# A new order list and a new list of PSUM tiles for an attention and expert kernel

## The chip, the cores and the metric

The kernel runs on one core of one Trainium2 chip. The metric is the device time of one execution in microseconds, as the median of the runs; a second kind of run records a profile, and all rows below come from one such execution.

## The reference, cut to what matters

Four batches with eight heads, 768 tokens, 64 numbers per head. Queries and keys are hashed to six bits with a common projection; a query sees only the keys whose six bits equal its own. The masked softmax attention of the 32 heads is put side by side to rows x of 512 numbers. Then, in each batch, the 128 tokens with the largest score x . w_gate pass through an expert (512 to 1024, relu, 1024 to 512), weighted with the sigmoid of the score, and are added to their own rows.

```python
q_bits = (np.einsum('bhsd,dk->bhsk', q, proj) > 0)
mask = q_bucket[:, :, :, None] == k_bucket[:, :, None, :]
scores = np.where(mask, scale * q @ k.T, -1e9)
out = softmax(scores) @ v
...
top_idx = np.argpartition(-(x[b] @ w_gate), capacity)[:capacity]
ye = np.maximum(xe @ w1, 0.0) @ w2
out[b, top_idx] = xe + sigmoid(score) * ye
```

## The kernel before

The whole program is written out as a list of words (ORDER). A loop at the end of `body` takes them one after the other; a word `name.h.i` calls one small function, for example `s.5.2` the score matmuls of head 5, unit 2. Each call puts its instructions behind those already in the queue of its engine, so the list fixes the sequence of every engine (TensorE, VectorE, ScalarE, GpSimd) and of both DMA queues in use (SP and ScalarE's own). Engines wait for each other by semaphores where data or a buffer asks for it; nothing is reordered when it runs. Words `w`, `c0` to `c3`, `e0` to `e3` each run a generator on to its next `yield`: weight loads, the choice of the tokens of a batch, the expert of a batch.

A second list, BANKS, gives to each new PSUM tile, in the sequence of the words that ask for one, one of four places: three tiles of two banks (numbers 0 to 2) and one of a single bank (3). Large results (max words, score words with even unit, hashes) need two banks, the others fit anywhere. A matmul that writes into a place waits until its last user has been read.

What the words do, by head h:

- `X` loads the transposed queries and keys (SP; the first two heads half by SP and half by ScalarE's queue), `xh` (ScalarE, L431) and `xl` (VectorE, L436) split them into two float16 parts. `V` loads values (ScalarE's queue), `vh` and `vl` split them. `lp` loads the projection and `pq` (VectorE, L336) splits it.
- `hx` (head 0, L382) and `h` (the others, L349) are hash matmuls; `sx`, `sg` take signs; `hs`, `dd` place signs and rows into the tile A for head 0, `ps` and `pa` do it by DMA on SP for the others (L443). `pb` copies into the tile B by DMA on SP. A has five buffers and B four, so `pa.h` and `ps.h` wait for the last score matmul of head h-5, `pb.h` for that of head h-4.
- `kv` (VectorE, L555) subtracts halves of the keys, `mx` (TensorE, L563), `re` (ScalarE, L570), `ma` (TensorE, L579) and `rd` (VectorE, L589) find the maximum of each query's scores. `mt` (TensorE, L597) transposes the maxima, `mc2` (ScalarE, L602) copies them, `mr` (SP, L443) writes them as a row into A. For head 0 `rt` and `rk` do this without a DMA.
- `s` (TensorE, L623 and L626) are the score matmuls, six units per head, and need the row; `e` (ScalarE, L639, L643) is the exponential; `r` (VectorE, L656) or `g` (GpSimd, L659) take the part that bfloat16 lost; `a` (TensorE, L683), six per head, multiplies with the values, 18 matmuls each.
- `rc` and `nw` (VectorE, L693 to L721) normalise, `sv`, `sh`, `sl`, `sa`, `sk`, `sd` prepare the start value of the sums. `sc` computes gate scores of the last batch.
- `c0` to `c2`: scores on VectorE, a transpose on TensorE, a copy, store and load back through HBM on SP (`sbc`), ranks by comparing, `idx` (VectorE, L848) and an indirect gather by GpSimd (L853). `c3` does the last batch without HBM.
- `e0` to `e2`: transposes of the gathered rows (TensorE, L875), up matmuls (L915; a step has 12), relu (ScalarE L926, VectorE L927, called htl), down matmuls (L937), the weighted sum (L949) and a scatter (L953). `e3` is the same for the last batch, fed by a selection with matmuls (L1073); `zh` and `zl` (VectorE, L1103) split x for it.
- `wu.30` (L273) are 30 matmuls on constants, `wl` (L1108) four on weights; their results are not used.

How the list before came about does not stand in the kernel; no cost and no due time is part of the program.

Of the kernel before, what the change touches and what calls it, by code (L numbers as in the profile page):

```python
# [52 lines left out]
rd.1.0 e.0.1 s.0.0 s.0.2 s.0.3 vh.1 ps.3.1 mt.1 e.0.0 e.0.2 pb.1.0 mc2.1 vl.1 X.4 ps.3.0 s.0.4 kv.2 e.0.3 mx.2.2  # L53
e.0.4 mx.2.1 s.0.5 r.0.0 a.0.0 w pb.1.1 w re.2.1 mr.1 mx.2.0 a.0.1 ma.2.1 re.2.2 ma.2.2 X.5 e.0.5 s.1.5 kv.3
rd.2.1 pa.3.0 rd.2.2 X.6 X.7 re.2.0 pb.2.3 xh.4 pb.2.2 pb.3.2 pb.3.3 e.1.5 g.0.1 pa.4.0 ma.2.0 s.1.2 pb.3.0 w sv.1
ia.4 mx.3.2 rd.2.0 a.0.2 wl.1 r.0.2 pb.2.1 xh.5 re.3.2 e.1.2 ma.3.2 s.1.0 sh.1 pb.2.0 sa.0 xl.4 sl.1 rd.3.2 xh.6
a.0.3 e.1.0 sk.0 s.1.3 mt.2 xh.7 mc2.2 w xl.5 a.0.4 mr.2 mx.3.1 re.3.1 xl.6 s.1.1 s.1.4 e.1.1 xl.7 r.1.0 w ma.3.1
e.1.4 h.1.0.4 e.1.3 pa.4.1 rd.3.1 a.0.5 mx.3.0 s.2.1 s.2.3 V.2 sg.1.0.4 ss.1.0.4 pa.5.1 re.3.0 e.2.1 rc.0 s.2.2
nw.0 e.2.3 g.1.1 ma.3.0 pb.4.2 w sd.1 rd.3.0 w s.2.5 s.2.0 ps.4.1 pa.5.0 mt.3 e.2.2 a.1.0 e.2.5 a.1.1 s.2.4 w
ps.4.0 ps.6.1 pb.3.1 kv.4 mc2.3 r.1.2 X.8 mx.4.0 mr.3 e.2.0 re.4.0 sa.1 a.1.2 sk.1 mx.4.1 X.9 X.10 ps.5.1 a.1.3  # L60
ma.4.0 a.1.4 re.4.1 ps.5.0 ma.4.1 pb.5.3 r.2.0 w e.2.4 rd.4.0 rd.4.1 a.1.5 xh.8 mx.4.2 pb.5.1 s.3.4 pa.6.0 rc.1
g.2.1 vh.2 s.3.2 re.4.2 ps.7.0 ma.4.2 s.3.5 ps.7.1 nw.1 e.3.4 sd.2 rd.4.2 pa.6.1 kv.5 r.2.2 s.3.0 e.3.5 s.3.3
# [1105 lines left out]
```

## Time and profile before

| | |
|---|---|
| median of 3 runs | 403.53 us (402.72 to 405.96) |
| profiled execution, its own time | 402.91 us |
| its span, first to last instruction | 401.1 us |
| TensorE matmul busy | 380.8 us (95%) |
| VectorE busy | 346.2 us (86%) |
| ScalarE busy | 304.1 us (76%) |
| GpSimd busy | 122.9 us (31%) |
| DMA | 53.82 MB moved, 134 GB/s on average |

Busy time of TensorE counts a matmul until its result is out, and matmuls overlap; so a busy engine can still run with gaps between the starts of its matmuls. Times in the rows are microseconds from the start of the span, durations are microseconds or, in groups, nanoseconds for one instruction.

### The profile page before, as it was taken

The page shows a single profiled execution, that of the slowest core. Times are in us where ns is not written, and L with a number is a line of the kernel's source. Part 1 is how long each engine was busy: PE and PEld are TensorE (multiplying, and loading weights), DVE is VectorE, ACT ScalarE, POOL GpSimd, SP SyncE. Part 2 cuts the span into 40 slices and gives each one's busy share as a digit, 9 for nine tenths or more (in the row PEclk, how much of TensorE's full clock was granted, in tenths as well). Part 3 has the DMA queues.
Part 4 walks back from the last instruction along what each step waited for, and adds up shares of the span by engine and source line. Part 5 has one row for each costly group of instructions (what it writes and reads, how often), then busy time and mean ns, then how long its engine had stood idle before and what let it go on. Part 6 is the DMA issues. An engine that isn't in the chain of part 4 may idle for free. (4 is left out here: it accounts for less than half of the span.)

```text
span 401.1 us, 13734 instructions
## 1 busy us (share of the span) xinstructions
PE 380.8 (95%) x5769; PEld 273.8 (68%) x5775; DVE 346.2 (86%) x580; ACT 304.1 (76%) x483; POOL 122.9 (31%) x80
## 2 busy tenths in 40 slices
PE   1989999999999999899999999999999999999996
PEld 0555677667666867578766677688576776779794
DVE  2779889998998999968899999987989998989942
ACT  3599998978898999779876997958667787784210
POOL 1004335223325234433142224222225235142010
PEclk9999999999999999999999999999999999999999
DMA  7467666475663654473573744332526442020210
GB/s 224 120 193 204 190 193 189 142 195 167 187 203 105 190 167 111 133 210 107 157 239 94 186 113 116 84 80 69 147 59 210 119 115 79 22 82 2 80 50 32
DMA packets 33191, 53.82 MB, mean 134 GB/s; under 512 B 5311, under 2 KB 24266, under 8 KB 33130
## 3 DMA queue, kind: packets, MB, share of 16 engines
q1 hardware_dynamic: 22480, 33.71, 30.2%
q10 hardware_dynamic: 10010, 17.15, 14.0%
q0 software_dynamic: 640, 2.10, 1.7%
q8 instruction: 45, 0.74, 0.8%
q14 instruction: 16, 0.13, 0.1%
HBM read 26.29 MB, written 7.35 MB: 84 GB/s over the span
## 5 line engine op out<-in xcount | busy, mean ns | idle before, releaser
L659 POOL TENSOR_TENSOR R<-P 128x1536 f16<-128x1536 f32 x32 | 88.0, 2749 | 149.5 <-DVE rc L693 34.7
L683 PEld LDWEIGHTS <-P 128*128 128x128 bf16 x2304 | 116.6, 97 | 14.2 <-issue 0.8
L683 PE MATMUL av<-V,P 128*128 128x65 f16 (+1 forms) x2304 | 122.3, 193 | 0.0
L683 PE MATMUL av<-V,R 128*128 128x65 f16 x1152 | 118.0, 192 | 0.3 <-DVE R L656 0.3
L656 DVE TENSOR_TENSOR R<-P 128x1536 f16<-128x1536 f32 x64 | 111.7, 1763 | 0.7 <-ACT P L639 0.6
L643 ACT ACTIVATE P<-two 128x1024 f32<-128x1024 f32 x96 | 97.0, 1022 | 17.5 <-PE two L626 15.1
L683 PEld LDWEIGHTS <-R 128*128 128x128 f16 x1152 | 105.5, 98 | 0.6 <-DVE R L656 0.6
L589 DVE TENSOR_REDUCE m<-two 128x2 fp32r<-128x770 f32 x96 | 89.9, 952 | 13.8 <-PE two L579 11.6
L623 PE MATMUL two<-A 97*128 97x512 f16 (+1 forms) x278 | 93.8, 347 | 1.5 <-DMA A<-mr 0.9
L626 PE MATMUL two<-B 128*128 128x512 f16 (+1 forms) x278 | 93.8, 346 | 0.0
L570 ACT ACTIVATE two<-two 128x770 f32<-128x770 f32 x96 | 75.3, 796 | 9.8 <-PE two L563 8.8
L623 PEld LDWEIGHTS <-A 97*128 97x128 f16 x384 | 37.7, 98 | 27.4 <-DMA A<-mr 3.9
L626 PEld LDWEIGHTS <-B 128*128 128x128 f16 x384 | 37.6, 98 | 23.8 <-issue 3.0
L579 PE MATMUL two<-A 96*128 96x385 f16 x192 | 46.9, 327 | 1.2 <-ACT two L570 0.8
L563 PE MATMUL two<-kd,A 96*128 96x385 f16 x192 | 45.4, 326 | 1.1 <-DVE A L427 0.7
L639 ACT ACTIVATE P<-one 128x512 f32<-128x512 f32 x53 | 31.4, 593 | 7.3 <-PE one L626 7.1
L436 DVE SCALAR_TENSOR_TENSOR XL<-X,XH 128x768 f16<-128x768 f32 x32 | 30.2, 953 | 0.4 <-DMA B<-XL 0.2
L639 ACT ACTIVATE P<-two 128x512 f32<-128x512 f32 x43 | 25.2, 592 | 5.0 <-PE two L626 3.4
L623 PE MATMUL one<-A 97*128 97x256 f16 x106 | 26.3, 273 | 2.5 <-DMA A<-mr 2.4
L431 ACT ACTIVATE XH<-X 128x768 f16<-128x768 f32 x32 | 26.7, 837 | 2.4 <-DMA X<-in_qk_dram 2.3
L626 PE MATMUL one<-B 128*128 128x256 f16 x106 | 26.3, 273 | 0.0
L579 PEld LDWEIGHTS <-A 96*128 96x128 f16 x192 | 16.2, 97 | 11.0 <-issue 2.7
(154 smaller groups left out, 494.4 us busy)
## 6 DMA issues: line engine op xcount, KB each, us to landing
X<-in_qk_dram SPq DMA_DIRECT2D x30, 384.0 KB
V<-in_v_dram ACTq DMA_DIRECT2D x16, 384.0 KB
B<-XL SPq DMA_DIRECT2D x64, 96.0 KB
B<-A SPq DMA_DIRECT2D x64, 96.0 KB
A<-XH SPq DMA_DIRECT2D x62, 96.0 KB
out_dram<-x ACTq DMA_DIRECT2D x7, 768.0 KB
W<-in_w_dram ACTq DMA_DIRECT2D x8, 512.0 KB
sbc<-scores SPq DMA_DIRECT2D x3, 384.0 KB
```

Source lines behind the costliest of these rows:

```text
L436: mine(nc.vector.scalar_tensor_tensor(xl, st["X", h], XS, st["XH", h], op0=ALU.mult, op1=ALU.subtract))
L563: nc.tensor.matmul(pt[:, i, : HS + 1], a[0:96, 0, q0 : q0 + P], kd, start=True, stop=False, skip_group_check=True,)
L570: nc.scalar.activation(o, o, AF.Relu)
L579: nc.tensor.matmul(pt[:, i, : HS + 1], a[0:96, 0, q0 : q0 + P], a[0:96, 1, HS : S + 1], start=False, stop=True, skip_group_check=True,)
L589: nc.vector.tensor_reduce(st["m", h][:, 2 * t : 2 * t + 2], st["mx", h, t][:, :, : HS + 1], axis=AX.X, op=ALU.max)
L623: nc.tensor.matmul(o, a[:, 1, k0 : k0 + P], a[:, 0, q0 : q0 + n], start=True, stop=False,)
L626: nc.tensor.matmul(o, bt[:, 1, k0 : k0 + P], bt[:, 0, q0 : q0 + n], start=False, stop=True,)
L639: nc.scalar.activation(pp[:, :, 512:S], pt.rearrange("p (a b) -> p a b", a=2), AF.Exp, scale=ES)
L643: nc.scalar.activation(pp[:, :, 0:512], pt, AF.Exp, scale=ES)
L656: mine(nc.vector.tensor_tensor(**rest(h, g)))
L659: turn(nc.gpsimd.tensor_tensor(**rest(h, g)))
L683: nc.tensor.matmul(o[:, t, 0:n], l, vv[:, c, hh, v0 : v0 + n], start=False, stop=last and l is lo, skip_group_check=True,)
```

## The change

Only the two lists change. All functions and all instructions stay as they are. The new list holds the same 2032 words, each as often as before, in another sequence, and 398 new numbers of PSUM tiles. The author's words for it: order list and PSUM tile choice anew from a plan in which random DMA issues and operations are late.

Below stand the beginning of both lists, the stretch around the choice of batch 0, the end, one place in the middle of the new list, and the first line of each list of PSUM places.

```diff
-V.0 X.0 X.1 tl xh.0 lp i0 dd.0.0 dd.0.2 pq dd.0.3 vh.0 X.2 xl.0 vl.0 X.3 dd.0.1 hx.0.0 ia.0 hx.0.1 xh.1 hx.0.2
-pa.1.1 ia.1 sx.0 ir.0 xl.1 pb.0.2 V.1 xh.2 hs.0.0 wu.30 hs.0.1 xh.3 kv.0 h.0.1.2 pb.0.3 sg.0.1.2 pa.1.0 lc mx.0.1
-xl.3 mx.0.0 ss.0.1.2 ir.1 sv.0 ps.1.1 re.0.1 ps.1.0 re.0.0 pb.0.1 mx.0.2 xl.2 re.0.2 ma.0.1 ia.3 ia.2 rd.0.1
-pb.0.0 ma.0.0 rd.0.0 ma.0.2 mc rd.0.2 pa.3.1 sh.0 h.0.2.4 sg.0.2.4 pb.1.2 pa.2.1 pb.1.3 kv.1 w ss.0.2.4 rt.0 sl.0
-rk.0 mx.1.2 re.1.2 mx.1.1 mx.1.0 ps.2.1 re.1.1 ma.1.2 re.1.0 s.0.1 pa.2.0 ps.2.0 ma.1.1 rd.1.2 rd.1.1 ma.1.0
...
-re.12.0 sk.5 w pb.12.1 e.10.2 s.11.1 a.9.3 r.10.2 ma.12.0 s.11.5 a.9.4 rd.12.0 pb.14.2 re.12.1 a.9.5 c0 pb.12.3
-xh.16 e.11.5 g.10.1 e.11.1 rc.9 pa.15.0 s.11.2 ma.12.1 vh.6 nw.9 s.11.3 c0 pb.14.1 pa.14.0 rd.12.1 vl.6 sd.10
-e.11.3 s.11.0 kv.13 ps.14.1 X.18 a.10.0 mt.12 e.11.2 a.10.1 mx.13.2 mc2.12 mx.13.1 e.11.0 a.10.2 a.10.3 sv.6 c0
-re.13.1 ps.15.0 mx.13.0 r.11.0 re.13.2 xh.17 mr.12 ma.13.1 sh.6 a.10.4 kv.14 re.13.0 ma.13.2 xh.18 a.10.5 pb.14.3
-w ma.13.0 rd.13.1 sl.6 s.12.4 rd.13.2 s.12.5 pb.13.1 e.12.4 s.11.4 rc.10 s.12.0 nw.10 sd.11 pa.15.1 g.11.1 w
...
-a.29.4 a.29.5 zh.0 e.30.5 sa.15 e.31.5 sk.15 s.31.1 s.31.2 e.31.1 g.30.1 e.31.2 rc.29 nw.29 zl.0 sc.3.0.1.2 s.31.3
-r.30.2 e2 sd.30 e.31.3 s.31.0 e.31.0 a.30.0 a.30.1 a.30.2 a.30.3 a.30.4 a.30.5 r.31.0 rc.30 nw.30 e2 e2 e2 s.31.4
-g.31.1 e2 sd.31 e.31.4 sc.3.1.2.3 a.31.0 sc.3.1.1.2 r.31.2 a.31.1 a.31.2 a.31.3 a.31.4 a.31.5 sc.3.1.5.6 e2
-sc.3.1.0.1 sc.3.1.4.5 sc.3.1.3.4 rc.31 e2 c3 e2 e2 c3 c3 e2 nw.31 e2 e2 c3 c3 c3 e2 c3 e2 c3 c3 c3 c3 c3 e2 zh.1
-c3 c3 c3 c3 c3 c3 c3 c3 c3 c3 c3 c3 e2 e2 c3 c3 zl.1 e3 e2 c3 e3 c3 e3 c3 e3 e3 c3 e3 e3 c3 e3 wl.0 wl.2
+X.0 tl X.1 xh.0 i0 lp X.2 pq hx.0.0 dd.0.0 xl.0 dd.0.2 X.3 hx.0.1 ia.0 pb.0.2 ia.1 xh.1 xl.1 hx.0.2 dd.0.1 xh.2
+pa.1.1 dd.0.3 ir.0 pb.1.2 sx.0 hs.0.1 ia.2 xh.3 h.0.1.2 kv.0 ia.3 hs.0.0 xl.2 sg.0.1.2 ss.0.1.2 mx.0.0 pb.0.3
+mx.0.2 pa.1.0 mx.0.1 re.0.0 xl.3 re.0.2 ma.0.0 pa.2.1 ps.1.1 re.0.1 V.0 rd.0.0 wu.30 ma.0.1 kv.1 ps.1.0 h.0.2.4
+pa.2.0 lc sg.0.2.4 ma.0.2 rd.0.1 mx.1.2 pb.0.0 pb.0.1 ir.1 re.1.2 mx.1.1 pa.3.0 rd.0.2 vh.0 w ss.0.2.4 ma.1.2 mc
+re.1.1 rd.1.2 ps.2.1 rt.0 ma.1.1 mx.1.0 ps.2.0 vl.0 pb.1.3 rk.0 rd.1.1 V.1 sv.0 re.1.0 s.0.0 sh.0 pa.3.1 e.0.0
+s.0.5 ma.1.0 e.0.5 sl.0 s.0.1 kv.2 ps.3.0 w rd.1.0 e.0.1 sa.0 s.0.4 sk.0 mx.2.1 X.4 mt.1 mx.2.0 pb.1.1 e.0.4
...
+mr.11 pa.14.1 r.9.2 xh.17 r.10.0 a.9.2 s.10.4 re.12.0 c0 re.12.1 a.9.3 kv.13 c0 ma.12.0 a.9.4 a.9.5 rd.12.0
+ma.12.1 pb.14.0 s.11.5 w c0 rc.9 ps.15.0 s.11.0 e.10.4 vh.6 nw.9 e.11.5 mx.13.1 g.10.1 rd.12.1 ps.14.1 s.11.1
+sd.10 pb.14.2 r.10.2 e.11.0 re.13.1 mx.13.0 c0 a.10.0 mt.12 vl.6 mc2.12 e.11.1 pb.12.1 a.10.1 re.13.0 s.11.2
+e.11.2 r.11.0 s.11.3 a.10.2 pb.13.1 e.11.3 pb.13.3 ma.13.1 a.10.3 sv.6 ma.13.0 mx.13.2 c0 pb.12.2 w a.10.4 rd.13.1
+xh.16 mr.12 pa.15.1 pa.15.0 a.10.5 V.7 s.12.5 rd.13.0 re.13.2 ma.13.2 rc.10 sh.6 g.11.1 xh.19 sl.6 e.12.5 ps.15.1
...
+xl.20 s.16.2 a.15.3 mx.19.1 pb.18.1 sa.8 a.15.4 r.16.0 e.16.2 w e0 pb.17.1 pb.20.2 a.15.5 sk.8 h.5.0.4 pb.18.0
+re.19.1 mr.17 rc.15 ma.19.1 sg.5.0.4 e0 s.17.5 pb.20.0 pb.20.3 g.16.1 rd.19.1 X.25 s.17.1 ss.5.0.4 nw.15 e0 e.17.5
...
+s.31.3 zh.0 e.31.3 r.31.0 a.30.0 a.30.1 a.30.2 a.30.3 sc.3.0.1.2 a.30.4 s.31.5 a.30.5 e.31.2 rc.30 g.31.1 e.31.5
+s.31.4 e2 nw.30 e.31.4 e2 sc.3.0.3.4 e2 r.31.2 sd.31 e2 sc.3.1.4.5 sc.3.1.3.4 a.31.0 sc.3.1.2.3 sc.3.1.1.2
+sc.3.1.5.6 sc.3.1.0.1 a.31.1 a.31.2 a.31.3 a.31.4 a.31.5 e2 e2 e2 rc.31 e2 c3 zl.0 e2 c3 c3 e2 nw.31 e2 c3 zh.1 e2
+c3 e2 c3 c3 e2 c3 c3 c3 c3 c3 e2 c3 c3 c3 c3 c3 c3 c3 c3 c3 c3 c3 c3 e2 c3 e2 zl.1 c3 c3 e2 e3 e3 c3 wl.0 e3 c3 e3
+e3 w c3 e3 e3 c3 e3 wl.2
...
-2321032102 1032130210 3230312203 1021213023 0121302103 1301201320 3130230210 3010312023 1320023102 1013230213
...
+2120132120 1302302130 2321330232 1023213203 2031320132 1302130321 3032331220 1321201330 1123213201 2031230231
...
```

## Rows read from the trace of the kernel before

**Rows 1.** The page, busy us (share of the span) and number of instructions.
```profile
PE 380.8 (95%) x5769; PEld 273.8 (68%) x5775; DVE 346.2 (86%) x580; ACT 304.1 (76%) x483; POOL 122.9 (31%) x80
```
**Rows 2.** Waits of TensorE: engine, line, releaser: us in total, times, longest.
```profile
PE two L382 <- DVE pjh L336: 8.1, 1, 8.1
PE one L623 <- DMA A<-mr: 2.4, 4, 0.8
PE one L875 <- DMA xe<-out_dram,idx: 1.5, 2, 1.3
PE two L623 <- DMA A<-mr: 0.9, 1, 0.9
```
**Rows 3.** Timeline of VectorE, start: start us, us, instruction, count [idle before].
```profile
7.03 0.72 DVE L411 COPY A<-XH 32x768 f16<-32x768 f16 x2 [6.16 <-ACT XH L431]
7.82 0.20 DVE L336 TENSOR_SCALAR pjh<-pjt 128x64 f16<-128x64 f32 x1
...
8.70 0.96 DVE L436 SCALAR_TENSOR_TENSOR XL<-X,XH 128x768 f16<-128x768 f32 x1
...
12.58 0.36 DVE L555 TENSOR_TENSOR kd<-A 96x384 f16<-96x384 f16 x1
```
**Rows 4.** Timeline of ScalarE, start.
```profile
6.15 0.84 ACT L431 ACTIVATE XH<-X 128x768 f16<-128x768 f32 x1 [2.29 <-DMA X<-in_qk_dram]
```
**Rows 5.** Timeline of TensorE, start.
```profile
10.44 3.38 PE L273 MATMUL one<-ones 128*128 128x128 f16 x30
...
14.91 0.83 PE L563 MATMUL two<-kd,A 96*128 96x385 f16 x4
...
20.39 1.11 PE L563 MATMUL two<-kd,A 96*128 96x385 f16 x4
```
**Rows 6.** Windows, first 8 us: length, busy time by engine, clock, DMA share, GB/s.
```profile
0.00:8.00 8.00, 0.00 (x0) 0.00 (x0) 0.94 (x4) 3.34 (x5) 1.95 (x23) 1.00 0.79 219
```
**Rows 7.** Timeline of TensorE, transposes and first score matmuls of heads 10 and 13.
```profile
115.49 0.41 PE L597 MATMUL one<-identr,m 128*6 128x128 f32 x1
...
121.11 0.27 PE L623 MATMUL one<-A 97*128 97x256 f16 x1 [0.79 <-DMA A<-mr]
...
153.11 0.27 PE L623 MATMUL two<-A 97*128 97x256 f16 x1
```
**Rows 8.** Timeline of SP's queue, the row writes of heads 10 and 13.
```profile
117.09 0.71 SPq L443 DMA_DIRECT2D A<-mr  x1
...
150.44 0.74 SPq L443 DMA_DIRECT2D A<-mr  x1
```
**Rows 9.** Timeline of VectorE, idx of batches 0 and 1.
```profile
164.91 0.15 DVE L848 TENSOR_SCALAR idx<-one 128x1 int32<-128x1 f32 x1
...
245.33 0.15 DVE L848 TENSOR_SCALAR idx<-one 128x1 int32<-128x1 f32 x1
```
**Rows 10.** Timeline of TensorE, transposes of gathered rows, batches 0 and 1.
```profile
170.51 0.41 PE L875 MATMUL one<-cs,xe 128*128 128x128 f32 x2 [1.26 <-DMA xe<-out_dram,idx]
...
250.69 0.29 PE L875 MATMUL one<-cs,xe 128*128 128x128 f32 x1
```
**Rows 11.** Windows for L683 (value words): length, PE and PEld busy, clock, DMA.
```profile
360.00:380.00 20.00, 7.04 (x216) 6.83 (x216) 1.00 0.13 41
```
**Rows 12.** Timeline of VectorE, end.
```profile
374.56 0.17 DVE L1024 TENSOR_TENSOR sc<-sc,sc 128x6 f32<-128x6 f32 x1
375.35 0.69 DVE L927 SCALAR_TENSOR_TENSOR htl<-two,hth 128x512 f16<-128x512 f32 x1 [0.63 <-ACT hth L926]
...
382.29 1.75 DVE L1103 SCALAR_TENSOR_TENSOR B<-x,B 128x1536 f16<-128x1536 f32 x1
```
**Rows 13.** Timeline of TensorE, end.
```profile
382.42 2.84 PE L1073 MATMUL two<-sel,B 128*128 128x128 f16 x48
...
396.04 1.03 PE L1108 MATMUL one<-w1h 128*128 128x512 f16 x4
396.90 1.03 PE L1108 MATMUL two<-w1h 128*128 128x512 f16 x4
```

More of the change, by code (lines that the diff above doesn't have):

```diff
@@ L53 @@
[L53 to L62, printed above, removed]
@@ new lines @@
+kv.11 mc2.10 mr.10 c0 s.9.4 e.9.0 s.9.1 sd.8 e.9.1 h.3.0.4 X.18 e.9.2 pb.12.3 sg.3.0.4 ss.3.0.4 s.10.5 a.8.0
+pb.12.0 pb.11.0 ps.12.1 mx.11.1 ps.12.0 a.8.1 c0 vl.5 s.9.3 e.9.4 X.19 a.8.2 ps.13.1 e.10.5 re.11.1 e.9.3 s.10.0
+mx.11.0 e.10.0 re.11.0 a.8.3 s.10.1 X.20 pb.11.1 mx.11.2 e.10.1 r.9.0 ma.11.1 kv.12 ma.11.0 w rd.11.1 re.11.2
+a.8.4 rd.11.0 a.8.5 sv.5 ma.11.2 sh.5 rc.8 sl.5 pa.14.0 nw.8 mx.12.2 re.12.2 pb.13.2 sd.9 s.10.2 s.10.3 e.10.3
+e.10.2 ma.12.2 ps.13.0 V.6 rd.11.2 pa.13.1 a.9.0 mx.12.0 a.9.1 rd.12.2 c0 sa.5 mt.11 mc2.11 sk.5 mx.12.1 g.9.1
@@ new lines @@
+s.12.4 ps.14.0 w e.12.4 nw.10 s.12.1 s.11.4 rd.13.2 e.12.1 s.12.3 e.11.4 pb.13.0 pb.15.2 mt.13 s.12.0 e.12.3
+mc2.13 pb.14.1 pb.15.3 c0 sd.11 s.12.2 pb.14.3 kv.14 mr.13 e.12.0 pa.17.1 xl.16 r.11.2 mx.14.2 a.11.0 sa.6 a.11.1
+xl.17 e.12.2 xl.19 re.14.2 sk.6 pb.15.1 a.11.2 mx.14.1 r.12.0 X.21 X.22 mx.14.0 w re.14.1 a.11.3 ma.14.2 rd.14.2
+a.11.4 s.13.3 ma.14.1 re.14.0 g.12.1 a.11.5 pa.16.1 xh.18 w rd.14.1 vh.7 ma.14.0 s.13.2 pa.16.0 s.13.4 e.13.3
+rc.11 rd.14.0 e.13.2 nw.11 c0 c0 mt.14 mc2.14 s.13.0 e.13.4 xl.18 s.13.1 pa.17.0 c0 s.13.5 mr.14 kv.15 pb.16.2
@@ new lines @@
+a.13.4 pa.19.1 mr.15 e0 ma.16.1 rd.16.0 pb.17.3 a.13.5 ma.16.2 s.15.3 s.15.0 ps.17.0 rd.16.2 s.15.2 rd.16.1 rc.13
+pb.16.0 s.15.1 xh.22 e.15.3 e.15.0 s.15.4 pa.19.0 nw.13 e0 e.15.1 g.14.1 kv.17 e0 e.15.2 X.24 r.15.0 e0 sa.7
+pb.18.2 mx.17.0 e.15.4 sk.7 mt.16 e0 sd.14 r.14.2 w pa.18.1 mc2.16 e0 mx.17.2 re.17.0 w w e0 re.17.2 a.14.0
+mx.17.1 ma.17.0 rd.17.0 a.14.1 ma.17.2 mr.16 s.15.5 pb.19.0 re.17.1 vh.8 a.14.2 ma.17.1 kv.18 e.15.5 w g.15.1
+s.16.5 a.14.3 rd.17.1 s.16.1 a.14.4 s.16.3 rd.17.2 e.16.1 mt.17 e.16.5 mc2.17 mx.18.1 a.14.5 xl.22 s.16.0 vl.8
@@ new lines @@
+c1 mr.19 e.18.5 re.20.0 sv.9 c1 c1 s.19.0 e.18.3 ma.20.0 s.19.4 e.19.0 a.17.2 mx.21.1 rd.20.0 e.19.4 c1 a.17.3
+re.21.1 r.18.2 mt.20 pa.22.0 mc2.20 s.19.2 ma.21.1 s.19.1 sh.9 ps.23.0 g.18.1 pa.23.1 e.19.2 rd.21.1 a.17.4
+ps.22.0 sl.9 mx.21.2 pb.22.1 a.17.5 X.27 V.10 sa.9 mr.20 mx.21.0 e.19.1 rc.17 s.19.5 re.21.2 sk.9 nw.17 re.21.0
+ps.23.1 ma.21.2 sd.18 X.28 X.29 e.19.5 s.19.3 e.19.3 ma.21.0 rd.21.2 rd.21.0 a.18.0 vh.10 c1 pb.21.2 s.20.2 mt.21
+a.18.1 vl.10 pa.24.1 mc2.21 mr.21 a.18.2 kv.22 c1 e.20.2 pb.21.0 c1 s.20.0 c1 s.20.3 pb.23.3 pb.22.2 c1 a.18.3
@@ new lines @@
+re.26.2 rc.22 e1 r.23.2 mt.25 e1 ps.27.0 ma.26.1 pb.27.2 e1 xh.30 X.31 e1 pa.28.0 xh.31 nw.22 pb.27.3 rd.26.1
+mc2.25 ps.27.1 e1 sd.23 r.23.0 xl.30 s.24.4 kv.27 s.24.2 ma.26.2 e.24.4 pb.25.2 a.23.0 s.24.0 pb.27.1 pb.25.1
+e.24.2 s.24.5 V.13 xl.29 e1 pa.28.1 sa.12 pb.26.0 xl.31 e.24.0 rd.26.2 a.23.1 r.24.0 e.24.5 a.23.2 sk.12 s.24.3
+r.24.2 mr.25 e.24.3 mx.27.2 g.24.1 s.25.1 s.25.0 mt.26 re.27.2 pa.29.0 a.23.3 a.23.4 ma.27.2 e.25.0 a.23.5 e.25.1
+rc.23 rd.27.2 nw.23 h.7.0.4 mc2.26 sg.7.0.4 sd.24 mx.27.0 c2 pa.29.1 s.25.5 pb.28.2 mr.26 c2 s.25.2 pb.28.1
@@ new lines @@
+mx.30.0 a.27.2 e.28.2 sh.14 mx.30.2 mc2.29 mx.30.1 pb.29.3 re.30.0 r.27.2 a.27.3 r.28.0 sl.14 ma.30.0 re.30.2
+ma.30.2 rd.30.0 a.27.4 re.30.1 sa.14 a.27.5 ma.30.1 rd.30.2 sk.14 kv.31 mr.29 e2 pb.30.1 V.15 pb.31.3 s.29.2
+rd.30.1 rc.27 e2 nw.27 e.29.2 s.29.3 s.29.0 e.29.3 g.28.1 r.28.2 sd.28 mt.30 vh.15 mc2.30 s.29.4 pa.31.0 mx.31.1
+re.31.1 e.29.0 pb.31.0 sc.3.0.4.5 a.28.0 pb.30.0 a.28.1 s.29.5 sc.3.0.2.3 a.28.2 a.28.3 ma.31.1 e.29.4 vl.15
+e.29.5 mx.31.0 sc.3.0.0.1 re.31.0 a.28.4 mx.31.2 e2 rd.31.1 a.28.5 e2 ma.31.0 rc.28 re.31.2 rd.31.0 pb.31.2 s.29.1
```

160 lines of the change are left out of this document (69 added, 91 removed), and 6 rows, old and new, of the table BANKS.

## The prediction

> **What bounds the kernel now.** I read the page first: TensorE is busy 380.8 of 401.1 us [rows 1], so it leaves 20.3 us. The view of waits says where: 8.1 us pass before its first matmul [rows 2]; its last matmul ends at 397.9 [rows 13], 3.2 us before the end; so some 9.0 us of idle time lie in between. Of these 4.8 are waits for DMA: 3.3 for the row of maxima of a head (1.5 KB, written into A) and 1.5 for the gathered tokens [rows 2]. The reader is to see that no engine beside TensorE sets the pace in the middle: a new order can give back parts of 9.0 us there, shorten the start, and spoil the end, where ranking the last batch is a chain on VectorE. The amount of work can't change.
>
> **The change, part by part.** Both lists hold the same 2032 words, each as often, and the same 398 numbers of PSUM tiles; so no instruction is added or removed. All is distance: how much TensorE work stands between a producer and the matmul that needs it. I count that from the two lists with prices from rows: a max word (mx or ma) 0.33 (four matmuls of 385 columns, 0.83, are two words less overlap) [rows 5]; a score word 0.87 (four of 512 columns, by the distance of the last two warm groups) or half of it [rows 13]; a value word 0.56 (twelve in 7.04, tails taken off) [rows 11].
>
> *Start.* V.0 (393 KB) goes from the first place of ScalarE's queue to behind the first maxima. At 219 GB/s [rows 6] those bytes are 1.8 us, so X.0 and the projection can land 0 to 1.8 us earlier than the 6.15 at which the first XH starts [rows 4]. On VectorE three copies and pq stand between XH and XL (2.63 us, 7.03 to 9.66) [rows 3]; in the new list pq and one copy, so two copies (0.72) [rows 3] leave the way. The chain to kv.0 (12.94 at its end) [rows 3] thus comes 0.7 to 2.5 earlier; I take 1.6, the middle: 11.3. The 30 warm matmuls (3.38 us) [rows 5], which stood before the first max word, now stand behind ma.0.0. So: three mx.0 words 11.3 to 13.3, ma.0.0 to 13.9 (both at the slow rate, below), the warm matmuls to 17.2, then ma.0.1, h.0.2.4 (six matmuls, 1.0) and ma.0.2 to 18.9, where the first mx.1 starts. Before, it starts at 20.39, with the row transposes rt.0 (0.7) already done [rows 5]. That leaves 0.8; vh.0 (as long as XH, 0.84 [rows 4]), which now stands on ScalarE between the maxima of head 1, can eat all of it. I take **a gain of 0.5**, ends: 2.5 (the whole of the earlier start) and a loss of 1.0 (the warm matmuls less the 2.4 us for which TensorE waited there anyway).
>
> [...] Rows: the 30 warm matmuls of 128 columns are 113 ns apart and 48 later ones of the same width 59 [rows 5, 13]; four of 385 columns right after the warm ones already run at the fast rate. [...]
>
> *Row of maxima.* mt.h transposes on TensorE, ScalarE copies, SP issues the row, and the head's first score matmul waits for it. Head 10: 115.49 to 121.11, of which 0.79 idle; from the issue 4.02 [rows 7, 8]. Head 13 needed no more than 2.67 from its issue and waited for nothing [rows 7, 8]. The TensorE work between mt.h and the first score word was below 5.0 us for 14 of 31 heads; those that waited had 4.2 to 5.1. In the new list it is below 5.0 for 8. Scaled, 3.3 x 8/14 = 1.9 of waits stay; I add 0.4 because head 10 has but 3.3 and the row of head 17 is queued on SP behind pb.20.2, which waits for the last score matmul of head 16, and pb.18.0. **Gain 1.0**; ends 3.3 (no row waits) and a loss of 4.6 (third case below).
>
> *Gather.* From idx on VectorE to the transposes: 5.60 with a wait of 1.26, and 5.36 without one [rows 9, 10]. TensorE work behind the idx words of the three batches: 4.3, 4.6, 5.2 before, 5.3, 4.4, 5.0 after. Against a need of 5.1 to 5.4 that is 0.8 to 1.5 of waits, now 1.5: **gain 0.4**, ends 1.5 and a loss of 0.6.
>
> *SP's queue.* In the new list pb.12.1, pb.13.1, pb.13.3, pb.12.2 and mr.12 come behind the load of batch 0's scores (sbc), itself behind the landing of the store. Behind the transposes of those scores TensorE has 11.3 us until s.12. The way: about 1.0 to the store's issue, landing 2.7 to 4.0, five issues of 0.71, landing again [rows 7, 8]: 10.0 to 12.6. Cost 0 to 1.3; **I take 0.3**. Other moves of DMA issues I cost at nothing: the consumer of an X load stands 20.2 us of TensorE work behind it on average (17.9 before), that of a V load 9.0 (9.5), that of the last pb of a head 8.7 (7.8); without that cover each would cost up to a landing, 4.0.
>
> *PSUM tiles.* The single bank is taken 114 instead of 103 times. Work between two users of a tile averages 3.2 us in both lists: nothing, ends 1 us either way.
>
> *End.* Two words are placed worse. zl.0 (1.75) [rows 12] stands between the last scores and the htl of batch 2; VectorE idled there 0.63 until 375.35 [rows 12]. From 374.73 it now goes to 376.48: the ranking chain is 1.13 later. One more up step of batch 2 (12 matmuls at 59 ns, 0.71) stands behind the last value words and fills part: 0.42 is left. wl.0 (four matmuls, 0.86 from start to start [rows 13]) ran last of all, off the path; it now stands between the selection and the up matmuls of the last expert, where TensorE never waits: 0.86 on the path. **Loss 1.3**, ends 0 and 2.0.
>
> Sum on the profiled execution (402.91 us with a span of 401.1; 0.62 below the median of 403.53): 402.91 - 0.5 - 1.0 - 0.4 + 0.3 + 1.3 = **402.6**.
>
> **Rivals.** *Slack pays fully:* no row and no gather waits, the start takes its whole gain: 402.91 - 3.3 - 1.5 - 2.5 + 1.3 = 396.9. For it: mean work from mt.h to the first score rises from 5.9 to 6.6 us, from mx to ma from 2.15 to 2.40. Against: ten rows now stand less than 1 us ahead of their first score in the list (five before).
>
> *Rows late on SP (slower):* if SP runs no further ahead than the list, those ten heads (9, 12, 17, 18, 19, 23, 25, 28, 29, 30) each wait as long as head 10 did, 0.79: 7.9 - 3.3 = +4.6, which gives 402.91 + 4.6 - 0.5 - 0.4 + 1.3 = 407.9. It decides where a row is issued later than 2.7 to 4.0 us before its first score [rows 7, 8]. Against: in the old list head 10's row stands 0.88 ahead of its first score, yet it was issued 4.02 ahead.
>
> [...]
>
> That the order has no effect is no case: an engine executes its words in the list's sequence.
>
> **How the numbers follow.** Forecast 0.60, slack pays 0.20, rows late 0.12, clock late 0.08. A measurement here tells no less than 1% from no change: 399.5 to 407.6. With one end met alone the forecast runs from 400.3 (rows) to 404.1 (start); adding the near half of the outer cases gives 397.0 to 406.6. Faster: 0.20 and 0.02 of the forecast (two gains met at once), 0.22. Slower: 0.12 and 0.02 for a late clock with the worse end of the tail, 0.14. Same: 0.64.
>
> **What would show it.** Start: first matmul before 8.07 and first mx.1 between 18 and 20. Rows: TensorE's waits for DMA on A<-mr between 1.5 and 3, heads 10 and 17 among them. End: htl about 1.1 us later against the last value matmul, and wl.0 between the selection and the up matmuls. I am wrong if idle time of TensorE between its first and last matmul grows above 9.0, or if new waits for PSUM or for R appear, which my counts cost at nothing.

## The result, and the profile after

| | before | after |
|---|---|---|
| median | 403.70 us (20 runs) | 400.61 us (20 runs, 397.65 to 404.69) |
| ratio | | 0.9903, 95% interval 0.9875 to 0.9932 |
| profiled execution | 402.91 us, span 401.1 | 397.65 us, span 395.9 |

The change made the kernel faster by about 1%. The ratio and its interval leave out executions more than 1.5% above the fastest of their kernel (two of after's 20), the medians do not. The profiled execution of after is its fastest, so the traces differ by more (5.2 us) than the medians (3.1). Two cuts of the span, the last value matmul of head 0 and that of head 31, show where it went. Windows of before; columns: length, then busy time and count of TensorE, of its weight loads, VectorE, ScalarE, GpSimd, then granted clock, DMA share, GB/s:

```profile
0.00:42.07 42.07, 31.82 (x317) 18.75 (x318) 29.55 (x42) 31.27 (x47) 7.32 (x27) 1.00 0.66 189
42.07:372.68 330.61, 324.00 (x5158) 235.26 (x5162) 301.94 (x497) 267.61 (x428) 112.65 (x50) 1.00 0.47 134
372.68:401.10 28.42, 25.01 (x298) 19.75 (x296) 14.68 (x43) 5.18 (x9) 2.97 (x3) 1.00 0.17 57
```

The same cuts of after:

```profile
0.00:41.77 41.77, 31.60 (x317) 18.29 (x318) 29.61 (x42) 31.43 (x47) 7.27 (x27) 1.00 0.70 199
41.77:365.61 323.84, 321.39 (x5149) 234.51 (x5151) 301.56 (x496) 268.25 (x428) 115.56 (x50) 1.00 0.47 136
365.61:395.90 30.29, 25.73 (x310) 20.69 (x308) 16.46 (x44) 5.28 (x9) 2.97 (x3) 0.98 0.16 53
```

Start -0.30, middle -6.77, end +1.87: together -5.20. An up step of 0.72 (12 matmuls) moved from the middle to the end; without it the middle gains 6.05 and the end loses 1.15. TensorE's idle time in the middle (length less busy) falls from 6.61 to 2.45, its busy time, the moved step left out, by a further 1.89. (The clock of 0.98 in the last stretch of after is a fall behind TensorE's last matmul, which ends at 391.8: 0.94 from 394 to 395 us, 0.50 from there to the end.)

TensorE's waits in the middle, before (us in total, times, longest):

```profile
PE one L623 <- DMA A<-mr: 2.4, 4, 0.8
PE one L875 <- DMA xe<-out_dram,idx: 1.5, 2, 1.3
PE two L623 <- DMA A<-mr: 0.9, 1, 0.9
PE two L623 <- ACT P L639: 0.4, 1, 0.4
PE av L683 <- DVE R L656: 0.3, 2, 0.2
PE two L563 <- DVE kd L555: 0.2, 1, 0.2
PE two L811 <- DVE m L589: 0.2, 1, 0.2
PE two L623 <- DVE m L589: 0.2, 1, 0.2
```

and after (its lines are those of before plus one):

```profile
PE one L624 <- DMA A<-mr: 1.0, 1, 1.0
PE two L876 <- DMA xe<-out_dram,idx: 0.9, 1, 0.9
PE two L580 <- ACT two L571: 0.2, 1, 0.2
```

Rows 3.3 to 1.0, gathered tokens 1.5 to 0.9, all others 1.3 to 0.2. The 13 waits before are 3 now. A wait costs more than its idle time: matmuls of 385 columns start 0.16 apart but each takes 0.33 until its result is out, so the first one behind a wait loses its overlap as well. Ten waits fewer at 0.16 are 1.6 of the 1.89 in busy time (an estimate). The starts in the two traces bear it out: over the 13 waits of before, the next matmul starts 8.2 us in all behind the spacing that is usual for a pair of these shapes (6.1 of it idle), over the 3 of after 2.2 us (2.1 idle). The difference, 6.0, is as much as the middle gains.

TensorE after, single rows that answer to [rows 5, 7, 10]:

```profile
11.65 1.60 PE L564 MATMUL two<-kd,A 96*128 96x385 f16 x6 [0.34 <-DVE A L395]
...
13.76 1.84 PE L274 MATMUL one<-ones 128*128 128x128 f16 x30
...
17.94 0.81 PE L564 MATMUL two<-kd,A 96*128 96x385 f16 x4 [0.49 <-DVE m L590]
19.31 0.49 PE L580 MATMUL two<-A 96*128 96x385 f16 x2 [0.56 <-ACT two L571]
...
20.88 0.49 PE L580 MATMUL two<-A 96*128 96x385 f16 x2 [0.72 <-ACT two L571]
...
116.62 0.28 PE L624 MATMUL one<-A 97*128 97x256 f16 x1 [0.97 <-DMA A<-mr]
...
167.74 0.30 PE L876 MATMUL two<-cs,xe 128*128 128x128 f32 x1 [0.88 <-DMA xe<-out_dram,idx]
...
201.50 0.27 PE L624 MATMUL two<-A 97*128 97x256 f16 x1
```

SP's queue after, the row writes of heads 10, 12 and 17 [rows 8]:

```profile
113.01 0.71 SPq L444 DMA_DIRECT2D A<-mr  x1
...
138.37 0.75 SPq L444 DMA_DIRECT2D A<-mr  x1
...
198.94 0.72 SPq L444 DMA_DIRECT2D A<-mr  x1
```

The reader is to see three things. The fast spacing is there before the warm matmuls: matmuls of 385 columns start 0.32 apart up to 12.59 and 0.16 behind it, and the 30 take 1.84 us where the same 30 took 3.38 [rows 5]. Head 10 alone waits for its row, though it was issued 3.61 ahead; head 17, which the prediction had wait, was issued 2.56 ahead and did not, nor did head 12 (first score at 140.68, 2.31 behind its issue). And first max word to first mx.1 takes 6.3 us against 5.5 [rows 5], so much of the earlier start is eaten on the way, where the waits at 17.94, 19.31 and 20.88 stand: the first max word comes 3.3 us earlier than before, the first scores 0.6 (22.36 for 22.92), the last value matmul of head 0 0.3.

### The profile page after: what moved, and what is told of

Same layout as the page of the kernel before. It is cut to its first block, busy times and chain, and to the rows that moved or that the text cites. A ratio compares the mean times of both kernels' runs of the same rounds, so it can differ in the third digit from the quotient of the medians.

```text
span 395.9 us, 13738 instructions
## 1 busy us (share of the span) xinstructions
PE 378.7 (96%) x5771; PEld 273.5 (69%) x5775; DVE 347.6 (88%) x580; ACT 305.0 (77%) x483; POOL 125.8 (32%) x80
## 4 chain that ended last, share of the span: by engine, by line
PE 77%; DVE 9%; DMA 6%; issue 4%; ACT 2%; SPq 0%; POOLq 0%; ACTq 0%; DVEq 0%
PE av L684 24%; PE two L624 12%; PE two L627 11%; PE two L580 7%; PE two L564 7%; PE one L624 3%; PE one L627 3%; PE one L938 3%; DMA xe<-out_dram,idx 2%; PE one L916 2%; DVE R L657 2%; PE two L350 1%; DMA pjt<-in_pj_dram 1%; DVE cm L778 1%; DVE m L590 1%
## 5 line engine op out<-in xcount | busy, mean ns | idle before, releaser
L660 POOL TENSOR_TENSOR R<-P 128x1536 f16<-128x1536 f32 x32 | 89.0, 2780 | 148.9 <-DVE R L657 28.0
L657 DVE TENSOR_TENSOR R<-P 128x1536 f16<-128x1536 f32 x64 | 113.6, 1790 | 0.7 <-ACT P L640 0.7
L437 DVE SCALAR_TENSOR_TENSOR XL<-X,XH 128x768 f16<-128x768 f32 x32 | 31.6, 1002 | 0.1
```

Source lines behind the costliest of these rows:

```text
L437: mine(nc.vector.scalar_tensor_tensor(xl, st["X", h], XS, st["XH", h], op0=ALU.mult, op1=ALU.subtract))
L657: mine(nc.vector.tensor_tensor(**rest(h, g)))
L660: turn(nc.gpsimd.tensor_tensor(**rest(h, g)))
```

## The experiments

The theory from the two traces: the gain is distance along the whole middle, the start gives nearly nothing, the end costs 1.2. Rivals: the start or the clock gives it; chance; one place. Each ratio is to executions of the kernel before taken along with the run, so between runs the ratios are to be compared.

**The changed kernel again, and with the old start.** The second kernel takes the old list as far as its word a.0.5 and then all words not yet used, in the new sequence (the cut shows it in short; a word that stands several times counts each time):

```diff
- ORDER = new
+ ORDER = old[:195] + [w for w in new if w not in old[:195]]
```

> The changed kernel once more, unchanged, as the measure for the other runs. Theory (the gain is distance in the middle, about 6 us on the profile, and a loss of 1.2 at the end): time 0.985 to 0.993 of the kernel before; TensorE's idle time between its first and last matmul 5.5 to 7 us (9.0 before), its waits for the row of maxima 0.5 to 1.5 us (3.3 before), for the gathered tokens 0.5 to 1.3 (1.5 before). Rival (the profiled execution was a lucky one and the order gives nothing): ratio 0.995 to 1.005 and idle time in the middle of 8 us or more.

> The old list up to the last value word of head 0 (195 words), then the new list's sequence for all the rest. Theory (the start gives only 0.3, the gain is made behind it): between 0.0 and 0.8 us slower than the changed kernel, a.0.5 done 0 to 0.6 later than 41.77. Rival (the gain starts at the start: V.0, the warm matmuls and the clock): 1.5 to 3 us slower than the changed kernel, so the ratio to the kernel before lies at 0.995 to 1.0.

Measured on the same chip: again 399.26, ratio 0.9880 (0.9836 to 0.9923); with the old start 398.78, ratio 0.9862 (0.9820 to 0.9904). So the gain is there again, and no part of it that these runs resolve comes from the start: with the old one the kernel was not slower, as the theory had it, and head 0 is done at 41.91. The repeat's profile has spans of 41.97, 324.38 and 30.25 for the three stretches: start 0.2 and middle 0.5 longer than the first profile.

That the middle is shorter by more than chance is seen in all profiles, these and some from further below, that leave its sequence alone (from the last value matmul of head 0 to that of head 31):

| profile | middle, us | waits of TensorE | idle in them, us |
|---|---|---|---|
| before | 330.61 | 13 | 6.1 |
| before, one warm matmul | 331.40 | 14 | 6.5 |
| before, start filled | 332.23 | 17 | 6.8 |
| after | 323.84 | 3 | 2.1 |
| after, again | 324.38 | 4 | 2.5 |
| after, old start | 325.01 | 4 | 3.0 |
| after, one warm matmul | 325.59 | 6 | 2.8 |

The granted clock is full in the middle of all seven. The least distance between the two groups is 5.0 us, 4.3 without the moved step.

**The old list for the first half** (1,199 words, to a.16.5), the same construction.

> The old list up to the last value word of head 16 (1,199 words, done at 221.3 us in the trace of before), then the new list's sequence for the rest. Theory (the gain is many small waits for rows, gathered tokens and PSUM tiles along the whole middle: 3.6 us of it lie before this point, 2.5 behind it, and the end gives back 1.2): 2.5 to 4.2 us slower than the changed kernel, ratio to the kernel before 0.994 to 1.000. Rival (one place makes the gain, behind the cut): within 1.5 us of the changed kernel.

406.19, ratio 1.0064 (1.0028 to 1.0099): slower than the kernel before, outside what both theories gave. Part of it is the clock (below): its mean was low in 10 of the 12 executions, in 14 of the 35 of before beside them, and the two at full clock, 404.54 and 402.48, are no slower than before at full clock (403.5). The trace shows the rest. From the last value matmul of head 18 to that of head 31, in this kernel, in before and in after:

```profile
245.38:373.97 128.59, 128.51 (x2143) 95.90 (x2144) 116.58 (x206) 96.45 (x154) 41.38 (x16) 1.00 0.32 93
```

```profile
241.18:372.68 131.50, 129.80 (x2152) 96.56 (x2156) 118.94 (x207) 96.23 (x153) 42.51 (x16) 1.00 0.32 90
```

```profile
237.24:365.61 128.37, 128.23 (x2141) 95.98 (x2144) 116.52 (x206) 96.59 (x154) 41.41 (x16) 1.00 0.32 93
```

There the new list gives its 2.9 us (0.72 of it the moved step) behind the old first half too. But the seam costs as much. From the cut to the last value matmul of head 18, with the same words at both ends but for one max word, this kernel and before:

```profile
223.18:245.38 22.20, 20.17 (x330) 14.33 (x330) 20.08 (x40) 17.61 (x28) 5.15 (x2) 1.00 0.39 117
```

```profile
221.25:241.18 19.93, 19.75 (x331) 14.51 (x331) 19.69 (x40) 17.77 (x28) 5.39 (x2) 1.00 0.55 142
```

TensorE waits there for a relu and for maxima (0.94, 0.79 and 0.30). From the cut to the last value matmul of all, this kernel takes 150.79 us and before 151.42: the moved step, and nothing more. The start, besides, ran 2.3 us longer than in the trace of before. So one place behind the cut does not make the gain, but neither does the second half by itself. In the trace of after the gain lies on both sides, 3.6 us up to the last value matmul of head 18 and 2.4 behind it. Whether the seam's price is that of the cut or of what the old first half leaves late, no run tells.

**Three waits taken out of the old list.**

```diff
- s.10.1 s.10.0 c0 r.9.0 mx.11.2 w a.8.2
+ c0 r.9.0 mx.11.2 w a.8.2 s.10.1 s.10.0
- s.29.3 a.27.3
+ a.27.3 s.29.3
- e0 r.13.2 mt.15 ... a.13.0 s.14.4 a.13.1
+ r.13.2 mt.15 ... a.13.0 s.14.4 a.13.1 e0
```

> The kernel before with three small moves and nothing else of the change: the first two score words of head 10 behind one more value word and one max word, the first score word of head 29 behind one value word, the transposes of the gathered tokens of batch 0 behind two value words and a score word. In the trace of before TensorE waited 0.79, 0.39 and 1.26 us there. Theory (a wait removed by distance comes back one to one, and distance is what the new list has more of): these three waits are gone from the trace, TensorE's lag behind its own work is 2.0 to 2.4 us smaller at the last value matmul, time 1.2 to 2.4 us less than before, ratio 0.994 to 0.997. Rival (the waits move to the next row or tile, because VectorE and ScalarE are as late as before): the lag falls by less than 1 us, ratio 0.998 to 1.002.

403.22, ratio 0.9979 (0.9947 to 1.0012). Its waits in the middle:

```profile
PE one L619 <- DMA A<-mr: 1.1, 2, 0.6
PE two L575 <- ACT two L566: 0.9, 2, 0.7
PE av L679 <- ACT av L536: 0.7, 1, 0.7
PE one L871 <- DMA xe<-out_dram,idx: 0.6, 1, 0.6
```

The three waits, 2.4 us, are gone as rows, but the relu ahead of `ma` (0.9), a start value of the sums (0.7) and batch 2's gather (0.6) make TensorE wait; the middle is 330.27 us long, 0.3 less than in the trace of before. It is tempting to say that the wait moved on to the next late producer. But a run with the old middle word for word (one warm matmul, below) has a relu's waits (1.3) and batch 2's gather (0.6) too: such waits come and go between executions of one list. Against the three old middles of the table this one is 0.3 to 2.0 us shorter, and by the ratio the run is 0.9 us faster than before, with an interval from 2.1 faster to 0.5 slower. So neither the theory nor its rival is settled; that the whole gain adds up from single waits is shown by the two traces and not by this run.

**The end.** Moving the two words that the prediction charged:

```diff
- ... c3 zl.0 e2 ...      ... c3 wl.0 e3 c3 e3 ...
+ ... zl.0 rc.30 ...      ... c3 e3 c3 e3 ... wl.0 wl.2
```

> The changed kernel with two words moved: zl.0 from behind the last scores of batch 3 to just ahead of rc.30 (VectorE idled 1.55 us there), and wl.0 from between the selection and the up matmuls of the last expert to just ahead of wl.2 at the very end. Theory (the prediction's step: these two cost 0.4 and 0.86): 0.9 to 1.5 us faster than the changed kernel, and the ranking chain (htl to the last ranks) starts 1.0 to 1.2 us earlier against the last value matmul. Rival (the tail is bound elsewhere, by the up matmuls' data or the final stores): within 0.4 us of the changed kernel.

399.74, ratio 0.9889 (0.9848 to 0.9930): no gain against the changed kernel (0.9880 and 0.9903). First, wl.0. TensorE after, from the selection to the up matmuls:

```profile
377.84 1.50 PE L1074 MATMUL one<-sel,B 128*128 128x128 f16 x24
379.18 1.03 PE L1109 MATMUL two<-w1h 128*128 128x512 f16 x4
380.04 0.29 PE L1081 MATMUL one<-c,sel 128*128 128x1 f16 x6
380.20 1.00 PE L916 MATMUL two<-xth,w1h 128*128 128x128 f16 x15
```

and without wl.0 there (lines are after's less five):

```profile
378.27 1.50 PE L1069 MATMUL one<-sel,B 128*128 128x128 f16 x24
380.45 0.29 PE L1076 MATMUL one<-c,sel 128*128 128x1 f16 x6 [0.67 <-ACT xtl L887]
380.60 0.77 PE L911 MATMUL two<-xth,w1h 128*128 128x128 f16 x11
```

The matmuls for the token numbers wait for ScalarE's copy of the selection's last group, and in the new BANKS both have tile 3 (`one` in the rows). Before, the last group has a two-bank tile (`two`, [rows 13]) and nothing waits:

```profile
385.10 0.29 PE L1080 MATMUL one<-c,sel 128*128 128x1 f16 x6
```

wl.0 only stood in a wait that the tile numbers make: behind the start of the last group the token matmuls come 2.20 us with it and 2.18 without. Second, zl.0. VectorE and GpSimd after:

```profile
358.59 2.75 POOL L660 TENSOR_TENSOR R<-P 128x1536 f16<-128x1536 f32 x1 [4.60 <-ACT P L644]
...
360.61 1.01 DVE L736 CUSTOM_DVE_ANT_0 jks<-x,wgt 128x256 bf16<-128x256 f32 x1
```

and with zl.0 (L1099) moved:

```profile
358.20 1.75 DVE L1099 SCALAR_TENSOR_TENSOR B<-x,B 128x1536 f16<-128x1536 f32 x1
...
360.12 2.75 POOL L655 TENSOR_TENSOR R<-P 128x1536 f16<-128x1536 f32 x1 [5.81 <-DVE rc L689]
...
360.95 2.19 DVE L731 CUSTOM_DVE_ANT_0 jks<-x,wgt 128x256 bf16<-128x256 f32 x1
```

GpSimd's subtraction is made to wait, by a dependency in the code (`turn`), for the last VectorE operation marked with `mine`; with zl.0 ahead of it in the list it starts 1.53 later (0.3 of it because all of this run's end is later; the releaser that the profile names is the small operation right behind zl.0). VectorE's gate score (jks, 0.41 when alone) then meets it and ends only some 0.28 behind GpSimd's end, 2.19 long. What zl.0 gave was lost there: the rank sums start 9.64 behind the last value matmul instead of 9.69, where the theory had 1.0 to 1.2 earlier.

Then the old sequence for the last 115 words, from a.29.5 on, old tile numbers included:

> The new list up to the last value word of head 29, then the old list's sequence for the last 115 words (heads 30 and 31, the last batch's ranking and expert). From the last value matmul to the end before took 28.4 us and the changed kernel 30.3, of which 0.71 is an up step that only stands later. Theory (the end lost about 1.2 by zl.0 standing in VectorE's ranking chain; wl.0 cost nothing, since TensorE waits there anyway): tail 28.2 to 28.9, idle time of TensorE elsewhere as in the changed kernel, time 0.6 to 1.4 us less than the changed kernel. Rival (VectorE is the bound of the last 30 us and only moves its lateness, as when zl.0 alone was moved): the value matmuls of head 31 end later by as much as the tail is shorter, time within 0.4 us of the changed kernel.

398.52, ratio 0.9868 (0.9824 to 0.9912). The tail is 28.70 as the theory said, but the stretch from a.29.5 to a.31.5 is 14.47 instead of 13.24 (0.72 of it the up step); from a.29.5 to the end 43.17 against 43.51. So 0.3 is won, by the profile, and 0.8 (42.75) in that of the last kernel below, which has the same end: between the rival and the lower end of the theory. By the times it is not resolved (0.9868 against 0.9880 and 0.9903). The profiled execution was itself a long one, 402.57 us, with two falls of the clock ahead of this stretch.

**The warm matmuls and the clock.** One instead of 30, in the new and in the old list:

```diff
- wu.30
+ wu.1
```

> The changed kernel with 1 instead of 30 warm matmuls on constants (their results are not used). Theory (in the new start the clock rose at 12.59 us, before the warm matmuls, so they are dead work of 1.85 us, and the waits behind them for maxima take part of the saving): first mx.1 0.5 to 1.8 us earlier than 17.94, matmuls of 385 columns still 0.16 us apart, time 0.3 to 1.2 us less than the changed kernel. [...]

> The kernel before with 1 instead of 30 warm matmuls (their results are not used). In its trace these matmuls ended the slow part of the start, at 13.96 us. Theory (the rise needs TensorE's run of work, and the old start has little else before the scores; in the changed kernel without them the clock fell back at 20.6 us): matmuls of 385 columns 0.32 us apart until the scores, 10 to 20 of them, time 0.5 to 3 us more than before. Rival (the warm matmuls are filler in the old start as well): within 0.5 us of before or faster by up to 1.5 us, 385-column matmuls 0.16 us apart from 14 us on.

New list: 400.27, ratio 0.9899 (0.9867 to 0.9930), no gain. The first mx.1 came at 17.70, only 0.24 earlier, since TensorE waited elsewhere in their place (0.86 and 0.82), and its clock fell. Windows of this kernel (clock is the column before the last two):

```profile
18.00:20.00 2.00, 1.36 (x12) 0.79 (x10) 1.21 (x3) 1.75 (x3) 0.00 (x0) 1.00 0.72 178
20.00:22.00 2.00, 1.36 (x4) 0.41 (x3) 1.94 (x3) 1.18 (x2) 0.00 (x0) 0.66 0.64 230
22.00:24.00 2.00, 2.00 (x17) 0.82 (x17) 1.64 (x4) 1.08 (x2) 0.00 (x0) 0.50 0.89 255
```

Old list: 404.94, ratio 1.0036 (1.0006 to 1.0066), a loss of 1.4 us by the ratio (0.2 to 2.7), as the theory had it. Its matmuls of 384 and 385 columns stay 0.32 apart until 16.5 us, where before they were fast from 13.96 on; the fast spacing still comes ahead of the scores. In the old start it comes earlier with the warm matmuls. That they keep the granted clock up later is not shown: without them the mean granted clock was low (below 0.998) in 5 of 9 executions of the new list and in 2 of 12 of the old, with them in 11 of 26 and in 34 of 77. (The windows over the slow spacing of the start, 8 to 13.8 us of before, print a granted clock of 1.00, so a low mean tells of a later fall.)

The fall is no property of that edit. The kernel with three waits less has the start of before word for word, and in its trace:

```profile
24.00:26.00 2.00, 2.00 (x8) 0.85 (x7) 1.88 (x3) 1.95 (x3) 0.00 (x0) 0.52 0.63 206
26.00:28.00 2.00, 2.00 (x7) 0.80 (x6) 1.89 (x3) 0.87 (x2) 0.00 (x0) 0.62 0.76 208
```

Head 0's last value matmul came at 44.08 there, at 42.07 in before. TensorE waited 1.21 us just ahead of that fall,

```profile
22.57 0.49 PE L559 MATMUL two<-kd,A 96*128 96x385 f16 x2 [1.21 <-ACT A L422]
```

and 0.74 at the same place in the trace of before, where the clock stayed. All five profiles with this start, that with one warm matmul included, go the same way: no fall where the wait is 0.74 (three), a fall where it is 1.08 or 1.21 (two). In the new start it is not so plain: with waits of 0.49, 0.56 and 0.72 the clock stayed in after, with 0.38, 0.56 and 0.72 it fell at 22 us in the kernel with the old end. So one and the same list falls in some executions, and what decides it is open. By the mean granted clock of each execution counted in the ratios: 0.998 or more in 43 of 74 before (mean 403.5) and in 15 of 24 after (399.5); less in 31 (405.3) and 9 (401.0). The change is worth 4.0 and 4.2 us at like clock, and a fall about 1.5 to 2: the clock does not carry the gain.

**Filling the idle time of the start.** First a version with four moves, then one with 24 more warm matmuls:

```diff
- s.10.5 a.8.0 ... mx.11.1 ... a.8.1      - e0 a.13.0 ... a.13.1
+ a.8.0 ... mx.11.1 ... a.8.1 s.10.5      + a.13.0 ... a.13.1 e0
- rc.30 g.31.1 ... zl.0                   - vh.0 ... re.1.1 ... vl.0 ... rk.0 ... sv.0
+ g.31.1 zl.0 rc.30                       + re.1.1 ... rk.0 vh.0 ... vl.0 ... s.0.5 sv.0
```

> The changed kernel with four moves. (1) The first score word of head 10 behind two more value words and a max word (its row wait was 0.97). (2) The transposes of batch 0's gathered tokens behind two more value words (wait 0.5 to 0.9). (3) zl.0 ahead of rc.30, and GpSimd's part of head 31 (g.31.1) ahead of zl.0, so that GpSimd does not wait for zl.0 as it did in the run before. (4) In the start vh.0, vl.0 and sv.0 behind the second max word of head 1, so that ScalarE's relu of head 1 is not behind vh.0 (waits 0.56 and 0.73). Theory (each wait comes back one to one): waits 1 and 2 gone, 1.4 to 1.9; 0.3 to 0.7 at the end; 0.3 to 0.8 at the start; together 1.5 to 3.2 us faster than the changed kernel, ratio to the kernel before 0.978 to 0.985. Rival (what is left of the idle time moves to other waits): within 0.8 us of the changed kernel.

400.21, ratio 0.9905 (0.9875 to 0.9935): no gain. In its profile the middle is 322.77, 1.1 to 1.6 shorter than in the two profiles of the changed kernel, with both waits gone (0.97 and 0.88 in after), but its start is 44.28 long: scores began at 21.35 (22.36), then TensorE waited 0.92 and 1.00 us, and the clock fell at 26. In 9 of 12 executions the mean was below 0.998.

```diff
(the first two moves of above, and)
+ wu.6
  mx.1.2
  ...
+ wu.8
  ma.1.2
  ...
+ wu.10
  ma.1.1
```

> The changed kernel with the two row and gather moves of the run before (head 10's first score word and batch 0's transposes later) and 24 more warm matmuls in the start where TensorE waits: 6 ahead of the first max word of head 1, 8 and 10 ahead of two of its adds (0.35, 0.45, 0.56 us; waits of 0.49, 0.56 and 0.73 there). In the earlier traces the granted clock fell to 0.5 to 0.6 for 3 to 4 us between 20 and 30 us in some executions of either list and in others not, at a price of about 2 us. Theory (the idle time around 18 to 22 us is what brings the clock down, and matmuls that fill it hold it up): the clock is at full speed in this stretch in the profile and in more than three quarters of the executions (mean granted clock 0.998 or more; 15 of 26 so far for the changed kernel), the first scores start no more than 0.4 later, time 1.2 to 2.5 us less than the changed kernel. Rival (the fall does not hang on these waits): mean clock below 0.998 in a third of the executions or more, and only the two moves show, 0 to 1.5 us.

398.38, ratio 0.9865 (0.9825 to 0.9905); clock 0.999 or more in all 6 executions. The time the theory expected is not resolved: against the changed kernel (0.9880 and 0.9903) the intervals overlap. The filler stands in the waits, here the add at 20.77 (20.88 in after):

```profile
19.88 0.73 PE L270 MATMUL one<-ones 128*128 128x128 f16 x10
20.77 0.49 PE L576 MATMUL two<-A 96*128 96x385 f16 x2 [0.15 <-ACT two L567]
...
73.03 0.38 PE L620 MATMUL two<-A 97*128 97x512 f16 x1 [1.37 <-DMA A<-mr]
```

The last row took the gain of the two moves: head 10's and batch 0's waits are gone, but the row of head 5 was issued 1.26 later than in after (68.82 for 67.56), and the middle is as long as before that edit (324.11). This row waited in one more profile, 0.40 in that of the last kernel below, which has the same start and the same moves, and in no other of the new list; whether the filling or chance makes it late is open.

The same in the old list (14 ahead of mx.1.0, 4 ahead of ma.1.2), and all that helped in one:

> The kernel before with 18 more warm matmuls in its start: 14 ahead of the third max word of head 1, where TensorE waited 0.74 us in the trace of before and 1.2 us in the two runs with the same start whose clock fell at 24 us, and 4 ahead of the add that follows (0.2). Theory (the clock's fall is a matter of this idle time, in either list, and no part of what the change gives): mean granted clock 0.998 or more in nearly all executions (before: 0.996 or less in 27 of 60), time 0.5 to 1.5 us less than before, so that 2.5 to 4 us of the new list's gain remain against it. Rival (the falls in the old list have another cause, or the new list's gain is that it falls less often): clock as often low as before, time within 0.4 us of before.

> What helped, put together: the changed kernel with the 24 filling matmuls in the start, the two moves for head 10's row and batch 0's gathered tokens, and the old list's sequence for the last 115 words. Theory (the start keeps its clock, the end gives back 0.3 to 0.9): clock 0.998 or more in nearly all executions, 0.3 to 0.9 us less than the run with the filling matmuls alone, ratio to the kernel before 0.981 to 0.987. Rival (the end is bound by VectorE either way): ratio as with the filling matmuls alone, 0.9865, within 0.4 us.

Old list filled: 403.79, ratio 0.9979 (0.9945 to 1.0013); the clock was low in 1 of 12 executions, as expected, the time gain is not resolved. All in one: 397.84, ratio 0.9851 (0.9796 to 0.9906), the lowest median here. It beats the kernel before; against the changed kernel (0.9880 and 0.9903) the intervals overlap, so that is not shown. Its clock was low in 2 of 6 executions, not at full speed in nearly all as expected. Over the three kernels with a filled start that is 3 of 24, against 45 of 103 for the two kernels without filling: the filling helps, most clearly in the old list (1 of 12 against 34 of 77), but it does not settle the matter.

## Why the prediction was right or wrong, point by point

Direction and range were right, the size was not. The sum took 0.3 us off the profiled execution of before, as the difference of 1.9 of gains and 1.6 of losses, so that it pointed the right way at all was near to luck; measured were 3.1 us by the medians and 5.2 by the traces, and 402.6 was 2 us above the median. The middle was sized at -1.1 (rows -1.0, gather -0.4, SP's queue +0.3, tiles 0) and gave -6.05 in the traces, some -4 to -5 by the timed runs (3.1 by the medians or 4.0 at like clock, plus the 1.15 lost at the end, less the start's 0.3). Of the 5 us that the middle gave beyond the sum in the traces, 1.9 are overlap, 1.3 rows, 1.1 the waits for tiles and other engines, the rest small.

- *Start, -0.5:* -0.30 in the traces, nothing that the run with the old start resolves. XH started at 4.88 for 6.15, the first matmul at 6.85 for 8.07. That vh.0 could eat the lead was right: it stands on ScalarE from 19.29 to 20.13, ahead of the relu for which TensorE waited 0.72.
- *Rows, -1.0:* 2.3, and this step failed. "Scaled, 3.3 x 8/14 = 1.9 of waits stay" took the number of rows with less than 5.0 us of work in between as the measure of the waits; 1.0 stayed (with 0.4 more, 2.3 were expected), with head 10 as named and without head 17. Rows landed within 2.31 and 2.56 of their issue, below the 2.7 to 4.0 that the prediction used; the landing varies, and 3.61 was too little for head 10.
- *Gather, -0.4:* -0.6 (1.5 to 0.9), near.
- *SP's queue, +0.3:* nothing; head 12's row did not wait.
- *PSUM tiles, 0:* wrong in the middle and at the end. In the middle the waits for P, R, kd and m went from 1.3 to 0.2 (by order and tiles together; neither was tried alone; in the repeat one of 0.75 for P stands there, at 42.73). At the end the new numbers make the wait of 0.67 that wl.0 covers.
- *End, +1.3:* +1.15 without the moved step, but the larger part of it for another reason. zl.0: htl starts 3.83 behind the last value matmul, 2.68 before, 1.15 as worked out, 0.72 of it filled, so 0.4 is left. wl.0: its 0.86 is on the path, yet "where TensorE never waits" was wrong; without it TensorE waits 0.67 there and the end comes no earlier. So the other part is the wait that the tile numbers make (added up, not tried with other numbers).
- *Not in the sum:* the overlap that each wait destroys, 1.6 to 1.9, the largest term that was missing.

Of the rivals, *slack pays fully* (396.9) describes the profiled execution (397.65), the fastest of 20, not the median, and not for its reasons: a row and a gather still wait, and the start gave 0.3. *Rows late on SP* did not happen: none of the ten heads waited. *Clock late*, 0.08 of the chances, was the author's estimate of a start that stays slow until the scores; no run shows one. In after the fast spacing came 1.4 earlier than before (12.59 for 13.96), and with one warm matmul in the old list at 16.5. What the runs show in its place is a later fall of the granted clock, in either list, to 0.50 to 0.74 in windows of 2 us. The falls come behind waits (0.4 to 1.2 us each between 18 and 26 us, 2.7 ahead of the one at 45), but waits of 0.5 to 0.7 in after brought none.

What stays open: which of the 2032 places carry the rest of the middle's gain. It also stays open how much of it is the sequence and how much the tiles. The half behind the cut gives nothing by itself, seam included; the three waits taken out of the old list could not be told from the spread; and late producers and DMA issues move from run to run. What sets off the fall of the clock is open too.
